# A windowed and a linear attention on one core: the same instructions emitted in another planned order

## The chip, the cores and the metric

The kernel runs on one core of a Trainium2 chip. The metric is the device time of one execution in microseconds (us); the time given for a kernel is the median of its timed runs.

## The reference, cut to what matters

Two independent attentions over 2,048 tokens of width 640 (32 heads of 20) stand side by side in the output. A is a softmax attention in which each query sees itself and the 255 keys before it; B is a linear attention with the feature map phi. All inputs are bf16.

```python
def _A_ref(x, wqkv, wo):              # S = 2048, D = 640, H = 32, Dh = 20, W = 256
    q, k, v = split(x @ wqkv)
    scores = jnp.einsum("bhqd,bhkd->bhqk", q, k) * (Dh ** -0.5)
    mask = (idx[:, None] - idx[None, :] >= 0) & (idx[:, None] - idx[None, :] < W)
    p = _softmax(jnp.where(mask[None, None], scores, -1e9), axis=-1)
    o = jnp.einsum("bhqk,bhkd->bhqd", p, v)
    return merge_heads(o) @ wo
def _B_ref(x, wqkv, wo):
    phi = lambda t: jnp.where(t > 0, t + 1, jnp.exp(t)) + 1e-6
    pq, pk = phi(q), phi(k)
    kv = jnp.einsum("bhsd,bhse->bhde", pk, v)
    z = jnp.einsum("bhsd->bhd", pk)
    o = jnp.einsum("bhqd,bhde->bhqe", pq, kv) / (jnp.einsum("bhqd,bhd->bhq", pq, z)[..., None] + 1e-6)
    return merge_heads(o) @ wo
return jnp.concatenate([a, b], axis=-1)   # (1, 2048, 1280)
```

## The kernel before

**A list of small jobs and a planner.** `build` (L317) does not write instructions in the order in which they run. It makes some 700 jobs, each with a closure that emits its instructions, the engines that may do it with an estimated duration, the jobs it depends on, and a name. `Planner.run` (L156) then plays a simple model of the chip forward in time: each engine has a clock, `LAT` is added between engines, a DMA job has an issue time, a service time and a fixed latency (the `D_...` tuples, L356 on), and eight DMAs may be under way for each kind of queue. Whichever engine is free first takes, among its ready jobs, the one with the lowest key, and the closure is called, so the planner's order becomes the program's order on that engine. The keys are in the table `TUNE`: `"name"` is a priority, and `"@name"` is the earliest time in nanoseconds at which a DMA job may be planned. Three scalars in `PRM` belong to the rules: `pvw` (how long a PV job is held back for company), `look` (how far ScalarE looks ahead for an exp) and `slack` (added to each planned landing). On the chip there are no planned times: each engine runs its fixed list, and waits with semaphores for what an instruction reads or overwrites.

**The work of A.** The 512-token tiles t = 0..3 are loaded turned (features on partitions) by `load_x` (L476; one `dma_start_transpose` of 512x640, L491, called a turned load here, names ldxA1..3), tile 0 as four row blocks that TensorE turns. `proj` (L504) makes q{t}.{i} and k{t}.{i}, each five matmuls of 128x512 (L516); the odd heads are regrouped by small DMAs on GpSimd's queue (rl1, rl2: L548, L551). `proj_v` (L565) makes v{t}.{b}.{i} (five matmuls of 128x320, L578) and copies half of each pair to other partitions through two DMAs on SyncE's queue (sw, L590 on). `attn` (L605) makes the scores as units S{t}.{g}.{u}: 32 or 48 small matmuls (L647) into one four-bank PSUM tile, of which there is one; one exp on ScalarE reads it all (L663, 128x2048, or 128x1536 for S0.g.3), VectorE multiplies masks in (L675), and PV{t}.{g} (L701, 144 instructions with their weight loads counted for t = 0, 192 otherwise) sums up the four or five units of a group g. There are 76 units. Each next unit needs the PSUM tile, so it starts when the exp before it has read it. The results go to DRAM (ow), come back in another layout (osum, oc: `a_out`, L754), and oa{t}.{b}.{hf} multiplies them with wo (`finish_rows`, L735) and stores.

**The work of B.** kB{t}.{b}.{hf} (five 128x320 matmuls, L835) with an exp and two more operations for phi make the keys' features; ten groups G{c}.{hf} (16 matmuls each, L860) sum features against the tokens (xtok0..3, plain loads); z and zt (L896 on) make the normalisers; kv and kvwo (L952, L970) form the 640x640 product with wo, which goes through DRAM (kvw, kvr); qB{t}.{c} (L1015), den (L1027) and ob{t}.{b}.{hf} (L735) make the output. The weights wvB, wo6 and wo6b (L934, L941, L942; 0.80, 0.75 and 0.15 MB) take the buffers of xtok0, xtok1 and xtok2, so their loads are issued when the last G group in TensorE's order has used these.

**Rings.** The turned tiles of A and B share three boxes in the order in which the loads are written down (A0, B0, A1, B1, A2, B2, B3, A3 and ldy0..3, B's tiles loaded again for the queries), so a turned load waits in SyncE's queue for the last reader of the box that it takes. Warm fillers without a purpose in the result (L1061 at the start, twelve of L1063 with the lowest priority) are emitted where the planner finds TensorE free. PSUM has four slots "F" for everything but scores.

**A unit and its PSUM tile, as emitted** (L639 and L663):

```python
st["s"] = mk("s", [P, 4 * SWD], F32, "S", tag="S")
...
nc.scalar.activation(out=o_, in_=i_, func=ACT.Exp, scale=scale)
```

Of the kernel before, what the change touches and what calls it, by code (L numbers as in the profile page):

```python
# [7 lines left out]
P = 128  # L8
# [6 lines left out]
PRM = {"rq": "POOL", "pvw": 4091, "look": 4707, "slack": 696, "xm": 5}  # L15
TUNE = {
    "x0n0": -288357, "@x0n0": 600, "x0n1": 22049, "@x0n1": 1123, "x0n2": 41981, "@x0n2": 2434, "x0n3": 84061, "@x0n3": 119, "ld.wq0": 76083,
    "ld.wk0": 12236, "@ld.wk0": 6060, "ld.wq1": -35479, "@ld.wq1": 3681, "ld.wk1": 6066, "@ld.wk1": 6620, "ld.wv": -505446, "@ld.wv": 5636,
    "cq0": -84337, "cq1": 2724, "cq2": 44219, "cq3": -23187, "cq4": -420730, "ck0": 5696, "ck1": -64118, "ck2": 18670, "ck3": 29291, "ck4": -26858,
    "x0t0": -132897, "x0t1": -294040, "x0t2": -85730, "x0t3": -4915, "q0.0": 19248, "q0.1": 26432, "q0.2": -6686, "q0.3": 45970, "q0.4": -489536,  # L20
    "rl1.q0": -40785, "@rl1.q0": 16932, "rl2.q0": 54695, "@rl2.q0": 13518, "k0.0": -73776, "k0.1": -51790, "k0.2": 37394, "k0.3": 113822,
    "k0.4": 46053, "rl1.k0": -502673, "@rl1.k0": 30975, "rl2.k0": -49405, "@rl2.k0": 26708, "v0.0.0": -6929, "v0.0.1": 47622, "v0.1.0": -526600,
    "v0.1.1": -444090, "sw0.0": -61952, "@sw0.0": 10936, "v0.2.0": 10862, "v0.2.1": -501633, "v0.3.0": 40518, "v0.3.1": -71548, "sw0.1": -68807,
    "@sw0.1": 9193, "ld.wkB": 25497, "@ld.wkB": 23848, "ldxB0": -246197, "@ldxB0": 26131, "ldxA1": -59032, "@ldxA1": 15091, "kB0.0.0": -45974,
    "kB0.0.1": -446546, "kB0.1.0": -18749, "kB0.1.1": -31544, "kB0.2.0": -28401, "kB0.2.1": -58682, "kB0.3.0": -6118, "kB0.3.1": -486764,
    "q1.0": -75602, "q1.1": -34298, "q1.2": 92743, "q1.3": 61377, "q1.4": -456991, "rl1.q1": -18606, "@rl1.q1": 55172, "rl2.q1": -528074,
    "@rl2.q1": 73862, "k1.0": -3303, "k1.1": -483479, "k1.2": 42406, "k1.3": -33423, "k1.4": -34976, "rl1.k1": 11630, "@rl1.k1": 46441,
    "rl2.k1": 40373, "@rl2.k1": 4611, "v1.0.0": 24902, "v1.0.1": 75996, "v1.1.0": -55369, "v1.1.1": 2908, "sw1.0": -456214, "@sw1.0": 43512,
    "v1.2.0": -35867, "v1.2.1": -288257, "v1.3.0": 33377, "v1.3.1": 46161, "sw1.1": -34319, "@sw1.1": 53419, "ldxB1": -26199, "@ldxB1": 41031,
    "kB1.0.0": -113500, "kB1.0.1": -23254, "kB1.1.0": -28925, "kB1.1.1": 46817, "kB1.2.0": -483358, "kB1.2.1": 7107, "kB1.3.0": 16553,  # L30
    "kB1.3.1": -6454, "ldxA2": -86975, "@ldxA2": 44207, "q2.0": 51284, "q2.1": -37600, "q2.2": -6714, "q2.3": 60478, "q2.4": -65006,
    "rl1.q2": -16466, "@rl1.q2": 19526, "rl2.q2": -509535, "@rl2.q2": 30153, "k2.0": -33063, "k2.1": -456351, "k2.2": -81624, "k2.3": 47673,
    "k2.4": -2355, "rl1.k2": 127476, "@rl1.k2": 117376, "rl2.k2": -21923, "@rl2.k2": 72214, "v2.0.0": 37551, "v2.0.1": 18807, "v2.1.0": -421067,
    "v2.1.1": -36145, "sw2.0": -45842, "@sw2.0": 23643, "v2.2.0": 25454, "v2.2.1": -539290, "v2.3.0": -130767, "v2.3.1": 11608, "sw2.1": -38625,
    "@sw2.1": 27245, "ldxB2": -550245, "@ldxB2": 38750, "kB2.0.0": 100598, "kB2.0.1": 10322, "kB2.1.0": -9462, "kB2.1.1": -69461, "kB2.2.0": -110719,
    "kB2.2.1": 38546, "kB2.3.0": -87349, "kB2.3.1": -486127, "ld.woA": -54728, "@ld.woA": 27767, "ldxB3": 27036, "@ldxB3": 91221, "kB3.0.0": -453951,
    "kB3.0.1": -38228, "kB3.1.0": -24615, "kB3.1.1": -37138, "kB3.2.0": -29442, "kB3.2.1": -45218, "kB3.3.0": -13993, "kB3.3.1": -71775,
    "xtok0": 104034, "@xtok0": 10388, "xtok1": -16821, "@xtok1": 51509, "xtok2": -120603, "@xtok2": 36076, "xtok3": -197007, "@xtok3": 97651,
    "G0.0": 10547, "G0.1": -17739, "G1.0": -55082, "G1.1": -8864, "G2.0": -490163, "G2.1": -324802, "G3.0": -26464, "G3.1": -33272, "G4.0": -15409,
    "G4.1": -483548, "z": 16997, "zt": -471321, "ldxA3": -19285, "@ldxA3": 88410, "q3.0": -23726, "q3.1": -37994, "q3.2": 56848, "q3.3": -265204,  # L40
    "q3.4": 52841, "rl1.q3": -78551, "@rl1.q3": 24462, "rl2.q3": -10455, "@rl2.q3": 61591, "k3.0": -41972, "k3.1": -13087, "k3.2": 65456,
    "k3.3": -26454, "k3.4": -7302, "rl1.k3": -39963, "@rl1.k3": 180268, "rl2.k3": 57329, "@rl2.k3": 9912, "v3.0.0": 29050, "v3.0.1": -43769,
    "v3.1.0": -18803, "v3.1.1": -1031, "sw3.0": -8116, "@sw3.0": 47187, "v3.2.0": 53184, "v3.2.1": -33591, "v3.3.0": 10942, "v3.3.1": -84607,
    "sw3.1": -41924, "@sw3.1": 24173, "ld.wvB": -426561, "@ld.wvB": 145679, "ld.wo6": -39687, "@ld.wo6": 30114, "kv0": -51294, "kv4": -426176,
    "kvwo0.0": 122701, "kvwo0.1": 12241, "kvwo1.0": -101551, "kvwo1.1": 31130, "kvwo2.0": -11861, "kvwo2.1": 11563, "kvwo3.0": 107146,
    "kvwo3.1": 131618, "kvwo4.0": -11166, "kvwo4.1": -50861, "kvwo5.0": 55450, "kvwo5.1": -278982, "kvw": -6720, "@kvw": 112744, "kvr": 46418,
    "@kvr": 69351, "ld.wqB": -280019, "@ld.wqB": 64126, "ow0": -429736, "@ow0": 27062, "ow1": 93906, "@ow1": 67296, "ow2": 44109, "@ow2": 53571,
    "ow3": 53864, "@ow3": 102364, "osum0": -573874, "@osum0": 76330, "oc0": -88479, "@oc0": 22414, "oa0.0.0": -82090, "oa0.0.1": -17943,
    "store": -53603, "@store": 120847, "oa0.1.0": 107388, "oa0.1.1": 50337, "oa0.2.0": -3404, "oa0.2.1": 34788, "oa0.3.0": -4230, "oa0.3.1": 37536,
    "osum1": -38603, "@osum1": 136143, "oc1": 47960, "@oc1": 56532, "oa1.0.0": -16324, "oa1.0.1": 24478, "oa1.1.0": -6962, "oa1.1.1": -12310,  # L50
    "oa1.2.0": 19872, "oa1.2.1": 25087, "oa1.3.0": -438000, "oa1.3.1": 29423, "osum2": -17457, "@osum2": 114162, "oc2": 4253, "@oc2": 130803,
    "oa2.0.0": -13955, "oa2.0.1": 10901, "oa2.1.0": -495123, "oa2.1.1": -10320, "oa2.2.0": -364531, "oa2.2.1": -12125, "oa2.3.0": -553036,
    "oa2.3.1": 21611, "osum3": 42013, "@osum3": 80849, "oc3": 59899, "@oc3": 118912, "oa3.0.0": -55744, "oa3.0.1": -244782, "oa3.1.0": -196742,
    "oa3.1.1": 41674, "oa3.2.0": -40598, "oa3.2.1": -584, "oa3.3.0": -93513, "oa3.3.1": -62120, "ldy0": 796, "@ldy0": 131627, "qB0.0": 29481,
    "qB0.1": -10081, "qB0.2": -68216, "qB0.3": -6372, "qB0.4": -46422, "den0": -33393, "ob0.0.0": -31941, "ob0.0.1": 35471, "ob0.1.0": -528525,
    "ob0.1.1": -24391, "ob0.2.0": -36065, "ob0.2.1": 27561, "ob0.3.0": -27764, "ob0.3.1": -464803, "ldy1": -13798, "@ldy1": 133257, "qB1.0": 1053,
    "qB1.1": -36459, "qB1.2": -444342, "qB1.3": -435813, "qB1.4": 56456, "den1": -388121, "ob1.0.0": -37266, "ob1.0.1": -54446, "ob1.1.0": 46384,
    "ob1.1.1": 63708, "ob1.2.0": 61437, "ob1.2.1": 91909, "ob1.3.0": 13961, "ob1.3.1": 25475, "ldy2": -531291, "@ldy2": 179542, "qB2.0": -110948,
    "qB2.1": 4978, "qB2.2": 35459, "qB2.3": 45246, "qB2.4": -18854, "den2": 89974, "ob2.0.0": -169618, "ob2.0.1": 7409, "ob2.1.0": -7287,
    "ob2.1.1": 9127, "ob2.2.0": 29090, "ob2.2.1": 55666, "ob2.3.0": 3198, "ob2.3.1": 20750, "ldy3": -581352, "@ldy3": 90810, "qB3.0": -56384,  # L60
    "qB3.1": -40973, "qB3.2": -253517, "qB3.3": -69741, "qB3.4": -66337, "den3": 30737, "ob3.0.0": -325, "ob3.0.1": 5523, "ob3.1.0": 43879,
    "ob3.1.1": 53150, "ob3.2.0": -38432, "ob3.2.1": -4618, "ob3.3.0": -75801, "ob3.3.1": -132216,
}


def KEY(name, value):
    return value


class Op:  # L70
    def __init__(self, idx, engs, emit, key, deps, mode, slots, g, rel, name, dma, cls, earliest, ni):
        self.ni = ni
# [25 lines left out]
class Planner:  # L98
    def __init__(self, slots):
        self.ops = []  # L100
        self.slots = {k: 0 for k in slots}
        self.free = {}
        self.log = []
        self.mode = "f"
        self.net = {"HW": 0, "SW": 0}
        self.lands = {"HW": [], "SW": []}
# [1248 lines left out]
```

## Time and profile before

| | |
|---|---|
| runs | 269.05, 269.86, 270.78 us; median 269.86 |
| profiled execution | 268.76 us, of which the span from the first to the last instruction is 267.0 |
| granted TensorE clock, mean over the span | 0.983 |
| TensorE | 4,117 matmul records, 248.9 us busy; 4,147 weight-load records |
| ScalarE | 204 instructions, 199.6 us busy; of these 76 exps with 141.0 us |
| VectorE | 457 instructions, 181.4 us busy |
| GpSimd | 93 instructions, 40.3 us busy |
| DMA | 36.07 MB, mean 135 GB/s |
| first and last matmul | starts at 1.27 us; ends at 262.58 us |

Times are counted from the first instruction. "Idle before" is the time that an engine stood still just ahead of an instruction, and the releaser is what ended it. "Issue" means that the engine waited for nothing the profile shows. "q8 instruction" is the DMA queue that brings TensorE's instructions: 33 packets of 16 KB. A matmul with its weight load counts as two instructions in TensorE's stream, which has 8,294 of these. A granted clock of 0.50 in a window means that TensorE ran at half speed there.

### The profile page before, as it was taken

The numbers are of one execution on the slowest core, as the hardware profiler recorded it, in microseconds if no ns is written. First come the engines' busy times: TensorE is split into PE (matmuls) and PEld (weight loads), VectorE is DVE, ScalarE is ACT, GpSimd is POOL, SyncE is SP. The second block draws the span as 40 slices with busy tenths as digits, with TensorE's granted clock in tenths as the row PEclk, the third lists the DMA queues.
The fourth block names the chain that finished last, engine by engine and source line by source line (L and its number), as shares of the span: only waits on it lengthen the run. The fifth ranks groups of instructions, "written<-read, shape, count | busy, mean of one in ns | idle before, by whom it ended". The sixth has DMA issues, their size and how long they took to land.

```text
span 267.0 us, 9518 instructions
## 1 busy us (share of the span) xinstructions
PE 248.9 (93%) x4117; PEld 149.3 (56%) x4147; DVE 181.4 (68%) x457; ACT 199.6 (75%) x204; POOL 40.3 (15%) x93
## 2 busy tenths in 40 slices
PE   8999989999999959999999999799979998999993
PEld 4754546565564635546666666655445555565672
DVE  1576758887769865768644556488789768675850
ACT  3528577897999956899786898189997797966631
POOL 5064503303060600007200000000500000000000
PEclk9999999999999997999999999799999999999998
DMA  7974969299342990001958129153996523213423
GB/s 227 337 144 147 156 193 220 67 204 215 92 146 68 150 233 8 21 23 62 260 102 133 62 47 259 47 174 94 202 155 185 182 83 117 76 50 100 160 99 104
DMA packets 52948, 36.07 MB, mean 135 GB/s; under 512 B 31702, under 2 KB 51494, under 8 KB 52902
## 3 DMA queue, kind: packets, MB, share of 16 engines
q1 hardware_dynamic: 50198, 32.39, 50.4%
q0 software_dynamic: 2048, 2.63, 5.0%
q8 instruction: 33, 0.54, 0.9%
q10 hardware_dynamic: 656, 0.41, 0.5%
q14 instruction: 13, 0.11, 0.2%
HBM read 13.90 MB, written 10.26 MB: 90 GB/s over the span
## 4 chain that ended last, share of the span: by engine, by line
PE 85%; issue 4%; ACT 3%; DVE 2%; SPq 2%; DMA 2%; ACTq 0%
PE F L735 17%; PE F L516 14%; PE S L647 10%; PE F L835 9%; PE F L860 9%; PE F L578 8%; PE F L701 7%; PE F L1015 6%; ACT p L663 3%; DMA sw<-vt 2%; PE F L1027 2%; SPq L491 1%; PE F L1061 1%; PE F L952 1%; PE F L1063 1%
## 5 line engine op out<-in xcount | busy, mean ns | idle before, releaser
L663 ACT ACTIVATE p<-S 128x2048 bf16<-128x2048 f32 x76 | 141.0, 1855 | 33.5 <-PE S L647 32.1
L675 DVE TENSOR_TENSOR p<-p,strip 128x256 bf16<-128x256 bf16 (+2 forms) x140 | 49.3, 382 | 17.0 <-ACT p L663 16.0
L809 ACT ACTIVATE e<-F 128x320 bf16<-128x320 f32 (+1 forms) x52 | 25.3, 498 | 6.3 <-PE F L835 3.1
L835 PE MATMUL F<-wkB,xT 128*128 128x320 bf16 x160 | 28.6, 307 | 0.2 <-issue 0.2
L548 POOL DMA_DIRECT2D odd<-even x32 | 16.5, 522 | 80.2 <-ACT even L415 58.3
L417 DVE CAST osb<-F 128x320 bf16<-128x320 f32 x41 | 19.4, 487 | 13.3 <-PE F L735 11.3
L551 POOL DMA_DIRECT2D odd<-st x32 | 17.9, 566 | 69.1 <-DVE st L417 55.7
L578 PE MATMUL F<-wv,xT 128*128 128x320 bf16 x160 | 28.0, 303 | 0.2 <-DVE e L813 0.2
L735 PE MATMUL F<-woA,oc 128*128 128x320 bf16 x160 | 27.1, 306 | 0.1
L516 PE MATMUL F<-xT,wk 128*128 128x512 bf16 x93 | 25.0, 379 | 0.7 <-issue 0.5
L735 PE MATMUL F<-kvwo,pq 128*128 128x320 bf16 x160 | 24.9, 299 | 0.2 <-DMA kvwo<-kvd 0.2
L1015 PE MATMUL F<-xT,wqB 128*128 128x512 bf16 x89 | 23.3, 380 | 1.1 <-issue 0.9
L417 DVE CAST ost<-F 128x512 bf16<-128x512 f32 x21 | 13.9, 688 | 14.9 <-PE F L701 14.9
L860 PE MATMUL F<-pk,xtok 128*128 128x320 bf16 x160 | 24.0, 300 | 0.0
L701 PE MATMUL F<-p,sw 64*32 64x320 bf16 (+3 forms) x720 | 21.6, 254 | 2.5 <-issue 1.9
L516 PE MATMUL F<-xT,wq 128*128 128x512 bf16 (+1 forms) x99 | 23.0, 358 | 1.0 <-issue 0.8
L701 PE MATMUL F<-p,vt 64*32 64x320 bf16 (+3 forms) x720 | 21.8, 254 | 0.7 <-issue 0.7
L417 DVE CAST even<-F 128x512 bf16<-128x512 f32 x24 | 16.5, 689 | 7.3 <-PE F L516 7.2
L647 PE MATMUL S<-odd 20*64 20x320 bf16 (+4 forms) x720 | 16.9, 261 | 4.1 <-issue 3.9
L835 PEld LDWEIGHTS <-xT 128*128 128x128 bf16 x160 | 15.1, 100 | 9.0 <-issue 1.0
L735 PEld LDWEIGHTS <-pq 128*128 128x128 bf16 x160 | 15.2, 98 | 8.3 <-issue 0.8
L578 PEld LDWEIGHTS <-xT 128*128 128x128 bf16 x160 | 15.0, 99 | 8.2 <-issue 1.4
(88 smaller groups left out, 309.1 us busy)
## 6 DMA issues: line engine op xcount, KB each, us to landing
out_dram<-osb SPq DMA_DIRECT2D x32, 160.0 KB, 2.0
OD<-ost SPq DMA_DIRECT2D x32, 128.0 KB, 2.4
xtok<-in_B_x_dram SPq DMA_DIRECT2D x4, 640.0 KB, 5.8
oc<-OD SPq DMA_DIRECT2D x4, 640.0 KB, 5.3
odd<-even POOLq DMA_DIRECT2D x32, 48.0 KB, 6.3
sw<-vt SPq DMA_DIRECT2D x16, 87.0 KB, 3.7
odd<-st POOLq DMA_DIRECT2D x32, 32.0 KB, 3.3
wv<-in_A_wqkv_dram SPq DMA_DIRECT2D x1, 800.0 KB, 6.7
```

Source lines behind the costliest of these rows:

```text
L417: nc.vector.tensor_copy(out=dst, in_=src)
L516: nc.tensor.matmul(ps[:, a:b], lhsT=w[:, kt, i, :], rhs=xb["t"][:, kt, a:b], start=(kt == 0), stop=(kt == KT - 1))
L578: return lambda ps: nc.tensor.matmul(ps[:], lhsT=xb["t"][:, kt, bb * P : bb * P + P], rhs=rhs_(), start=(kt == 0), stop=(kt == KT - 1))
L647: nc.tensor.matmul(st["s"][64 * i : 64 * i + 64, o0 : o0 + b - a], lhsT=kb["t"][32 * j : 32 * j + Dh, sl, ko : ko + 64], rhs=qb["t"][32 * ...
L663: nc.scalar.activation(out=o_, in_=i_, func=ACT.Exp, scale=scale)
L675: nc.vector.tensor_tensor(out=x, in0=x, in1=mkv[:, None, :].to_broadcast([P, 4, 64 * w]), op=ALU.mult)
L701: nc.tensor.matmul(O[i][32 * j : 32 * j + 32, a:b], lhsT=lhsT, rhs=pb["t"][64 * i : 64 * i + 64, o0 : o0 + b - a], start=(cnt == 0), stop= ...
L735: return lambda ps: nc.tensor.matmul(ps[:], lhsT=lhs(c), rhs=rhs(c, hf), start=(c == 0), stop=(c == KT - 1))
L809: nc.scalar.activation(out=eb["t"][:, 0:n], in_=ps[:], func=ACT.Exp)
L835: return lambda ps: nc.tensor.matmul(ps[:], lhsT=xb["t"][:, kt, b * P : (b + 1) * P], rhs=R["wkB"][:, kt, hf * HALF : (hf + 1) * HALF], st ...
L860: return lambda ps: nc.tensor.matmul(ps[:], lhsT=R["xt", tb // 4][:, tb % 4, c * P : (c + 1) * P], rhs=R["pk", tb // 4][:, tb % 4, hf * HA ...
L1015: return lambda ps: nc.tensor.matmul(ps[:], lhsT=R["wqB"][:, kt, :].rearrange("p (f c) -> p c f", c=KT)[:, c, :], rhs=xb["t"][:, kt, :], s ...
```

## The change

Every emitted instruction and every transfer stays what it was: the same 8,294 loads and matmuls, 76 exps, 439 VectorE and 202 ScalarE operations of the planned jobs, and the same DMAs, 16 sw transfers on SyncE's queue in both. What differs is the order in which each engine gets them, since the planner has other numbers:

- the whole table `TUNE` (every priority and every earliest time), and `pvw`, `look` and `slack`;
- the model of transfers: one server for both kinds of queue instead of two, another landing formula, and other costs for every kind of DMA;
- sw is planned on SyncE's queue, where it was emitted before too, although the planner had it on GpSimd's; `load_x` loses a branch that was not taken; `heat` tells the planner its count of instructions.

```diff
-PRM = {"rq": "POOL", "pvw": 4091, "look": 4707, "slack": 696, "xm": 5}
+PRM = {"rq": "POOL", "pvw": 2241, "look": 3200, "slack": 509, "xm": 5, "sq": "SP"}
 TUNE = {
...
-DMA_LEAD, DMA_LANES = 700, 8
+DMA_LEAD, DMA_TAIL, DMA_LANES = 1190, 300, 8
...
-        self.net = {"HW": 0, "SW": 0}
+        self.net = 0
...
-                q = "SW" if e == "POOL" else "HW"
-                for _ in range(n):
-                    self.net[q] = max(done + DMA_LEAD, self.net[q]) + svc
-                    land = self.net[q] + fix - DMA_LEAD
-                    self.lands[q].append(land)
+                q = self.lands["SW" if e == "POOL" else "HW"]
+                for i in range(n):
+                    self.net = max(t + dur * i // n + DMA_LEAD, self.net) + svc
+                    land = max(self.net, t + dur * (i + 1) // n + DMA_TAIL) + fix
+                    q.append(land)
...
-    D_XT5 = (3500, 1, 4200, 1150)
+    D_XT5 = (2850, 1, 3300, 1800)
...
-        D_RL1 = (950, 1, 350, 2100)
+    D_RL1 = (520, 1, 708, 1106) if RQ == "POOL" else (740, 1, 540, 893)
...
+    SQ = PRM.get("sq", RQ)
+    D_SWAP = (560, 1, 560, 1100) if SQ == "POOL" else (630, 1, 419, 965)
...
-                        nc.sync.dma_start(out=sws[slot][64:128, :, :], in_=vts[slot][0:64, :, 336:684])
+                        q_of(e).dma_start(out=sws[slot][64:128, :, :], in_=vts[slot][0:64, :, 336:684])
...
-                o = dma(sw, D_SWAP, -4990, [...], name=f"sw{t}.{hb}", eng=RQ)
+                o = dma(sw, D_SWAP, -4990, [...], name=f"sw{t}.{hb}", eng=SQ)
```

The emitted orders compare as follows where they differ most. SyncE's queue, before: ..., ldxB1, ow, ow, ldxA2, xtok1, ow, ow, ldxB2, ow x4, oc0, osum0, ow, ow, ldxA3, ldxB3, ...; after: ..., ldxB1, ow, ow, xtok2, sw1.0, ldxB2, ldxA2, ow, ow, sw1.1, ow, ow, ldxB3, osum0, oc0, xtok1, ow, ow, xtok3, sw2.0 (first half), ow, ow, ldxA3, .... Near the end of B's sums both have wvB, wo6, wo6b in a row.

TensorE at the last G group, before: G0.0 (its long piece of 30 instructions starts at 157.33 us) with S2.3.0, z, S2.3.1, zt, pieces of tile 1's output projection, S2.3.2, PV2.2, kv4 and kv0; after: G4.0, G1.0, G3.0 with S2.3.3, S2.3.4 and S3.0.0 between their pieces, then S3.0.1, PV2.3, pieces of tile 1's output projection, S3.0.2, z, S3.0.3, kv0, zt, kv4. TensorE between S0.3.3 and S1.0.3, before: the rest of kB1.2.0, PV0.3, and projections of tile 2; after: PV0.3 and kB1.0.1 to kB1.3.1, with the first projection of tile 2 (k2.4) just behind S1.0.3. Over the whole stream the units come in the same sequence, and so do the PVs.

## The prediction

> **What bounds the kernel now.** First the page's shares, clock and chain.
>
> ```profile
> PE 248.9 (93%) x4117; PEld 149.3 (56%) x4147; DVE 181.4 (68%) x457; ACT 199.6 (75%) x204; POOL 40.3 (15%) x93
> PEclk9999999999999997999999999799999999999998
> PE 85%; issue 4%; ACT 3%; DVE 2%; SPq 2%; DMA 2%; ACTq 0%
> ```
>
> TensorE is the bound. With the same instructions in another order only three things can move the end: time in which TensorE stands ("issue" is 4% of the chain, 11 us), stretches of halved clock (the two 7s), and the waits that the order makes. Next the chain around the two longest halts (start, length, what):
>
> ```profile
> 97.25 0.21 PE S L647 x13
> 97.47 2.92 issue
> 100.39 0.36 PE S L647 x11
> ...
> 165.50 1.11 PE F L701 x78
> 166.61 1.92 issue
> 168.53 0.53 PE F L701 x16
> ```
>
> Both halts fall inside a row of like matmuls, so no tile is waited for. By count they stand before the 3,010th and the 5,570th instruction of TensorE's stream: exactly ten blocks of 256 apart, and q8 brings 33 packets for 8,294 instructions. I call every 256th place an edge. The transfers by queue (packets, MB, share of 16 engines), first in 85.8 to 97.4 us, then in 97.4 to 99:
>
> ```profile
> q1 hardware_dynamic: 5147, 1.31, 81.8%
> q0 software_dynamic: 255, 0.33, 16.8%
> q14 instruction: 2, 0.02, 0.8%
> ...
> q1 hardware_dynamic: 497, 0.49, 97.2%
> q8 instruction: 1, 0.02, 5.6%
> ```
>
> For 11.6 us q8 got nothing while the others filled the engines. TensorE passed the edge before at 92.65, which asks for the block wanted at 97.47; its packet ran from 97.46 for 1.44 us, and TensorE went on 1.5 us later. The other long halt is alike: packet wanted at about 163, started 165.98. Ahead of it stood three loads that SyncE issued together (1.7 MB):
>
> ```profile
> 157.94 0.38 SPq L934 DMA_DIRECT2D wvB<-in_B_wqkv_dram  x1
> 158.49 0.42 SPq L941 DMA_DIRECT2D wo<-in_B_wo_dram  x1
> 159.03 0.41 SPq L942 DMA_DIRECT2D wo6b<-in_B_wo_dram  x1
> ```
>
> By stage (window, length, PE, PEld, DVE, ACT, POOL busy, granted clock, DMA share, GB/s): each halt is followed by one window of 3.41 us at half clock.
>
> ```profile
> 97.69:101.10 3.41, 0.71 (x15) 0.45 (x16) 0.81 (x3) 0.33 (x2) 0.00 (x0) 1.00 0.71 254
> 101.10:104.52 3.42, 3.42 (x22) 1.76 (x27) 1.33 (x4) 1.92 (x2) 0.00 (x0) 0.50 0.03 8
> 165.96:169.37 3.41, 1.50 (x79) 1.04 (x64) 0.28 (x1) 1.83 (x1) 0.00 (x0) 1.00 0.24 70
> 169.37:172.78 3.41, 3.41 (x31) 2.96 (x29) 2.02 (x5) 0.00 (x0) 0.00 (x0) 0.50 0.25 82
> ```
>
> Last the score units, from ScalarE's timeline. One PSUM tile serves all 76, so a unit starts only when the exp before it is done:
>
> ```profile
> 53.13 1.88 ACT L663 ACTIVATE p<-S 128x2048 bf16<-128x2048 f32 x1 [0.46 <-PE S L647]
> 54.90 0.43 ACT L809 ACTIVATE e<-F 128x320 bf16<-128x320 f32 x1
> 55.76 1.88 ACT L663 ACTIVATE p<-S 128x2048 bf16<-128x2048 f32 x1 [0.42 <-PE S L647]
> ```
>
> From a unit's start to its exp 0.50, the exp 1.88, to the next unit 0.04 to 0.16: a cycle of 2.45 us (least seen 2.42 and 2.47; 2.02 with the 1.45 us exp of tile 0's narrow units). Here the starts are 2.63 apart: TensorE has enough between them.
>
> **The change, part by part.** I laid the changed order out with TensorE's durations from rows of before: a unit 0.43 us, five 128x512 matmuls 1.08, five 128x320 0.685, a PV 1.42 (tile 0: 1.035), z 1.23, a filler 0.22. This work is the same in both orders.
>
> *Edges moved.* Undisturbed, from an edge passed (209.79) to the block after it ready (212.95) takes 3.1 us. Before, the least work between edges is 2.47, 2.87 and 3.54 us, since they lie in a PV or unit (many short instructions). The halts at edges 11, 21, 25, 27 and 29 are 2.92 + 1.92 + 0.24 + 0.41 + 0.70 = 6.2 us. In the new order the least is 4.26. If every fetch ran at once, no halt would be left: −6.2.
>
> *A fetch behind queued loads.* In the nine cases of before in which transfers filled the engines, q8's packet started when those queued ahead had run. After, wvB, wo6 and wo6b are issued 0.6 us into the long piece of G3.0, as they were into that of G0.0; before, TensorE went on 168.53 − 157.33 = 11.2 us after that piece's start. Edge 22 now falls in PV2.3, behind the issue; its block is wanted at edge 23, the end of S3.0.3, after 7.76 us of work. A new halt of 11.2 − 7.8 = 3.4 us, in front of kv0, which needs wvB anyway. Bounds: 0 if the fetch is served between the loads, 5.0 if it waits for all of wo6b's landing (167.56). I take +3.4, as the old halt is the same three loads in the same order. The Trainium skill ("Runtime: NRT & Kernel Launch", section "Instruction fetch mechanics") agrees on blocks of 256 instructions but calls the crossing mostly hidden; the 2.92 and 1.92 above say otherwise, and by that sentence this term would be near 0.
>
> *Other edges behind transfers* (after edges 5, 7, 17 and 24, soon after a turned load's or several small transfers' issue): nothing to +2.5; +0.4, since a packet at 27.90, 1.6 us after the issue of a turned load (26.30), came without delay.
>
> *Half clock.* A window at half clock loses 3.41/2 = 1.7. Two before; one after, behind the halt of 3.4. −1.7. Idle of 0.88 in a window (193.26 to 196.67) halved nothing; idle of 1.91 and 2.70 did.
>
> *Score cadence.* Where TensorE's work between two unit starts is below the cycle, it waits. Before: S2.3.3 (1.67), S3.1.0 (2.30), S3.1.1 (1.57), S3.2.1, S3.2.2; shortfall 2.6 us. After: S0.2.2 2.19, S0.3.2 2.18, S0.3.3 1.39, S1.0.0 2.28, S1.0.1 1.67, S1.0.2 1.66 (only kB1 groups are at hand, as ldxA2 now stands behind ldxB2), shortfall 2.9; S3.0.4 2.28, S3.1.0 1.39, S3.1.1 2.12, S3.1.3 1.27, shortfall 2.7. Net 5.6 − 2.6 = +3.0, bounds +2 and +4.5 (phi's exps between: 0.43 each on ScalarE, where they don't fit). Behind a waiting unit stand the masks and the PV, which come two units later, so nothing else is late.
>
> *Transfers moved.* The wait for sw at 34.41 (0.63) goes, as sw now stands ahead of ldxB0 in SyncE's queue: −0.6. wk1 goes behind xtok0 (640 KB), with 3 us of cover; nothing, without cover at most xtok0's 2 us. ldxA2 behind ldxB2: k2.4 needs it 9.3 us of work later, and the cadence waits add 2; turned loads took 5.8 to 8.7 us alone, 10.1 to 12.5 in pairs: 0, at most +1. ldxA3 8.2 us ahead of q3.1: +0.2, at most +2. The last stretch and the tail (4.4 us after the last matmul) are alike.
>
> *Sum:* −6.2 + 3.4 + 0.4 − 1.7 + 3.0 − 0.6 + 0.2 = −1.5. The profiled execution (268.76, span 267.05) becomes 267.3, span 265.5. The runs' median lies 1.1 above that execution; on its scale I forecast 268.4.
>
> **Rivals.**
> *B: the fetch isn't held up by the 1.7 MB.* For: q8 is a queue of its own, with one packet at a time. Against: the nine late packets. Then 3.4 and the last half-clock window go: 268.4 − 3.4 − 1.7 = 263.3. The Trainium skill ("DMA: Bandwidth & Descriptors", section "Queues, rings and completion order") speaks for it: an engine takes turns between the queues that have work, a packet each. By that rule, 97.46 should have been 92.65; the trace disagrees at least there.
> *C: the fetches wait for turned loads too; slower.* Edge 5 comes 1.3 us after the issue of ldxB2, edge 7 1.8 us after that of ldxB3. If a fetch issued so shortly behind one starts at its landing (8.5 us after issue; up to 12.5 for the pair B2, A2), TensorE goes on 2.85 us after that: 52.7 + 8.5 + 2.85 = 64.05 against edge 6 at 59.77, 4.3 late; 65.1 + 8.5 + 2.85 = 76.45 against edge 8 at 73.29, 3.2 late. 268.4 + 7.5 = 275.9, one alone about 272.5 with a halved window. A packet more than 2.9 us behind edge 5 or 3.6 behind edge 7 becomes a halt; 4.0 behind both brings the kernel back to 269.9. For: a packet wanted at 56.2, with ldxA2 issued at 51.19, came at 60.49. Against: 27.90.
> *D: the halts are not the edges'* and stay with the work wherever it goes: only cadence and sw count, 269.86 + 3.0 − 0.6 = 272.3. Against: the exact 2,560 instructions.
>
> **How the numbers follow.** Forecast 0.46 (own range 266 to 271: the fetch's 0 to 5.0, the cadence's +2 to +4.5), B 0.26, C 0.20, D 0.08. One per cent, 2.7 us, is about what a measurement tells from no change: below 267.2 or above 272.6. Faster: 0.14 of the forecast's and 0.25 of B's, 0.39; slower: 0.02, C 0.16 and D 0.03, 0.21; same 0.40. The range 262 to 274 leaves out C's upper part (0.13) and B's lowest (0.04).
>
> **What would show it.** q8's packet about 8 us after wvB's issue and a halt of 2 to 5 us in front of kv0, with one 0.50 window behind it; no halt ending on "issue" above 0.5 us elsewhere; unit starts 2.45 apart with waits ahead of S1.0.2, S1.0.3, S3.1.1 and S3.1.4. Wrong if q8 keeps coming during the three loads (B), if a halt stands 256 instructions behind edge 5 or 7 (C), or if halts stand off the edges (D).

## The result and the profile after

| | before | after |
|---|---|---|
| runs, same job | 269.05 to 271.06, median 270.32 us | 266.28 to 267.09, median 266.98 us |
| profiled execution | 268.76, span 267.05 | 267.09, span 265.29 |
| last matmul ends | 262.58 | 259.63 |

The ratio is 0.9876 (95% interval 0.9831 to 0.9920): 1.2% faster. A second comparison on another chip gave 0.9893 (0.9833 to 0.9953). The forecast for the median was 268.4, inside a range of 262 to 274; 266.98 was measured, 1.4 us less. For the profiled execution it was 267.3, and 267.09 was measured. The kernel before spreads more from run to run (266.4 to 271.2 in the comparisons with other kernels below) than the one after (266.2 to 267.1), which is why the medians lie 3.3 us apart and the two profiled executions 1.7. Runs of a slower state, the longest at 273.6 us, are left out of these spreads and of all ratios.

The page after, in the same parts as before (line numbers are now those of the changed kernel: the scores' L647 is L635, the exp's L663 is L651):

```profile
PE 248.2 (94%) x4118; PEld 149.6 (56%) x4147; DVE 182.4 (69%) x457; ACT 198.7 (75%) x204; POOL 40.4 (15%) x93
...
PEclk9999999999999999999999999977999999999999
...
PE 84%; ACT 7%; issue 4%; DVE 3%; ACTq 0%; DVEq 0%
```

TensorE is still the bound and still 4% of the chain is "issue", but the two 7s of the clock now stand side by side: one place instead of two. The chain there (start, length, what):

```profile
172.88 0.43 PE S L635 x15
173.31 3.04 issue
176.35 0.42 PE S L635
176.77 0.65 PE F L723 x2
```

That is S3.0.3, held before its very last matmul. It is the only halt on "issue" above 0.2 us in the whole stream; before there were six, 6.45 us in sum. The transfers by queue (packets, MB, share of 16 engines) from wvB's issue on, 165.7 to 173.5 us, and then from 173.5 to 175:

```profile
q1 hardware_dynamic: 1328, 1.65, 86.0%
...
q1 hardware_dynamic: 404, 0.41, 91.7%
q8 instruction: 1, 0.02, 5.3%
```

Nothing came on q8 while nearly all of the three loads ran; its packet started at 173.58, which is 7.80 us after wvB's issue at 165.78 (8.04 before). The edge that asks for it, in PV2.3, was passed at about 168.7. The windows behind it (window, length, PE, PEld, DVE, ACT, POOL busy, granted clock, DMA share, GB/s):

```profile
172.57:175.99 3.42, 0.58 (x25) 0.31 (x24) 0.97 (x3) 0.26 (x1) 0.00 (x0) 1.00 0.81 204
175.99:179.40 3.41, 3.05 (x31) 2.54 (x31) 1.58 (x5) 1.88 (x1) 0.00 (x0) 0.50 0.04 11
179.40:182.82 3.42, 3.42 (x37) 2.35 (x36) 2.03 (x4) 1.75 (x1) 0.00 (x0) 0.50 0.17 51
```

Two windows at half clock follow the one halt, where one had been forecast. And the waits in front of score units, which the view of before does not have at all (engine, line, releaser: us in total, times, longest):

```profile
PE S L635 <- ACT p L651: 2.7, 7, 0.7
```

### The profile page after: what moved, and what is told of

The parts are those of the page before. It is cut to its first block, busy times and chain, and to the rows that moved or that the text cites. A ratio compares the mean times of both kernels' runs of the same rounds, so it can differ in the third digit from the quotient of the medians.

```text
span 265.3 us, 9525 instructions
## 1 busy us (share of the span) xinstructions
PE 248.2 (94%) x4118; PEld 149.6 (56%) x4147; DVE 182.4 (69%) x457; ACT 198.7 (75%) x204; POOL 40.4 (15%) x93
## 4 chain that ended last, share of the span: by engine, by line
PE 84%; ACT 7%; issue 4%; DVE 3%; ACTq 0%; DVEq 0%
PE F L723 17%; PE F L504 16%; PE S L635 9%; PE F L848 9%; PE F L566 9%; PE F L1003 7%; PE F L823 7%; PE F L689 6%; ACT p L651 6%; PE F L1015 2%; PE F L1049 1%; PE F L940 1%; ACT e L797 1%; PE F L1051 1%; DVE p L663 1%
## 5 line engine op out<-in xcount | busy, mean ns | idle before, releaser
L651 ACT ACTIVATE p<-S 128x2048 bf16<-128x2048 f32 x76 | 141.1, 1857 | 25.8 <-PE S L635 23.3
L663 DVE TENSOR_TENSOR p<-p,strip 128x256 bf16<-128x256 bf16 (+2 forms) x140 | 49.2, 381 | 17.4 <-ACT p L651 16.8
L823 PE MATMUL F<-wkB,xT 128*128 128x320 bf16 x160 | 26.7, 300 | 0.2 <-DVE p L663 0.2
L566 PE MATMUL F<-wv,xT 128*128 128x320 bf16 x160 | 26.4, 300 | 0.1
L1003 PE MATMUL F<-xT,wqB 128*128 128x512 bf16 x90 | 24.1, 380 | 1.1 <-issue 0.7
L504 PE MATMUL F<-xT,wq 128*128 128x512 bf16 (+1 forms) x99 | 24.0, 358 | 0.8 <-issue 0.3
L413 DVE CAST even<-F 128x512 bf16<-128x512 f32 x26 | 17.9, 689 | 9.0 <-PE F L504 8.3
L723 PE MATMUL F<-kvwo,pq 128*128 128x320 bf16 x160 | 23.9, 299 | 0.2 <-DVE pq L1034 0.2
L635 PE MATMUL S<-even 20*64 20x320 bf16 (+4 forms) x720 | 16.7, 263 | 5.7 <-issue 3.0
L723 PEld LDWEIGHTS <-oc 128*128 128x128 bf16 x160 | 15.3, 100 | 11.9 <-issue 4.7
L689 PE MATMUL F<-p,vt 64*32 64x320 bf16 (+3 forms) x720 | 21.1, 254 | 0.0
L566 PEld LDWEIGHTS <-xT 128*128 128x128 bf16 x160 | 14.8, 98 | 8.6 <-issue 1.2
```

The source lines that it names most:

```text
L413: nc.vector.tensor_copy(out=dst, in_=src)
L504: nc.tensor.matmul(ps[:, a:b], lhsT=w[:, kt, i, :], rhs=xb["t"][:, kt, a:b], start=(kt == 0), stop=(kt == KT - 1))
L566: return lambda ps: nc.tensor.matmul(ps[:], lhsT=xb["t"][:, kt, bb * P : bb * P + P], rhs=rhs_(), start=(kt == 0), stop=(kt == KT - 1))
L635: nc.tensor.matmul(st["s"][64 * i : 64 * i + 64, o0 : o0 + b - a], lhsT=kb["t"][32 * j : 32 * j + Dh, sl, ko : ko + 64], rhs=qb["t"][32 * ...
L663: nc.vector.tensor_tensor(out=x, in0=x, in1=mkv[:, None, :].to_broadcast([P, 4, 64 * w]), op=ALU.mult)
L689: nc.tensor.matmul(O[i][32 * j : 32 * j + 32, a:b], lhsT=lhsT, rhs=pb["t"][64 * i : 64 * i + 64, o0 : o0 + b - a], start=(cnt == 0), stop= ...
```

## The experiments

Theory 1: the next block of 256 instructions is asked for at an edge of TensorE's stream, its packet waits for the transfers queued ahead, and nearly all that the new order gains is that fewer edges meet such transfers. Its rivals: the halts belong to the work around them; q8 is served in turn; or the new order is better in itself.

Several kernels below keep one of the two orders and move single jobs in it. For that the planner's choices are collected, some are shifted, and only then emitted. An entry of `MOVES` such as `('ldxB3', 0, 'ow1', 3)` puts the first job named ldxB3 right behind the fourth one named ow1:

```diff
-            if not dry:
-                o.emit(e)
+            seq.append((o, e))
...
+        for what, nth, where, wth in MOVES:
+            x = seq.pop(find(what, nth))
+            seq.insert(find(where, wth) + 1, x)
+        if not dry:
+            for o, e in seq:
+                o.emit(e)
```

**after_edges_192: the edges moved, nothing else.**

```diff
-            for i in range(n * NQ // w):
+            for i in range(104 if w == NQ else n * NQ // w):
                 if w == NQ:
-                    nc.tensor.matmul(psum(g)[:], lhsT=warm[:, 0:P], rhs=warm[:], start=True, stop=True)
+                    nc.tensor.matmul(psum(g)[:, 0:39], lhsT=warm[:, 0:P], rhs=warm[:, 0:39], start=True, stop=True)
```

> The kernel after, with the eight warm-up matmuls of 512 columns cut into 104 of 39 columns: about the same warm-up work, 192 more instructions at the very start of TensorE's stream, so every 256-instruction edge falls 192 instructions earlier in the work (64 later by the next edge); nothing else is changed. Theory 1 (a block's fetch is asked for at the edge before and waits for the transfers queued ahead): an edge now lies ahead of wvB's effect differently, the next one comes later, in kv0, and the halt of 3.04 us at S3.0.3 becomes one of about 1.3 us (0.5 to 2) at kv0; too short to halve the clock, so both half-clock windows (1.7 us each) go: about 262 us. Rival (the halt belongs to the work around S3.0.3 or to the waiting for data): it stays at S3.0.3 with 3 us and the time at 267.

Measured: 263.98 us, ratio 0.9821 (0.9759 to 0.9882). From its chain:

```profile
175.29 0.54 PE F L940 x9
175.84 1.48 issue
177.32 0.54 PE F L940 x6
```

L940 is kv0: the halt left S3.0.3 and came to the place and nearly the size that theory 1 named (1.48 for 1.3). The profiled execution still had one half-clock window behind it, which I had not expected of so short a halt, and a second halt of 0.52 in a PV. 192 more small instructions in the warm-up made the median about 3 us less (2.4 less than in after_again below). By the ratios, into which the spread of the kernel before enters, it is 1.5 to 1.9 us, and their intervals overlap.

**after_wo_late: the suspected transfers taken away from ahead of the fetch.** `MOVES = [('ld.wo6', 0, 'ow2', 7)]`

> The kernel after, with the job that loads wo and wo6b (0.9 MB) put behind the next two ow transfers in SyncE's queue, so that only wvB (0.8 MB) stands ahead of the fetch that edge 22 asks for; TensorE's order and its edges are unchanged. Theory 1: the packet comes when wvB has run, about 5.1 us after its issue instead of 7.8, TensorE is held at S3.0.3 for 0.5 us (0 to 1) instead of 3.04, the two half-clock windows go, and kvwo may wait up to 1 us for wo: about 261.5 us. Rival (q8 is served in turn with the other queues, or the fetch is slow by itself): the packet still comes about 7.8 us after wvB's issue, the halt stays 3 us, 267.

Measured: 261.15 us, ratio 0.9733 (0.9670 to 0.9796), against 0.9876 for the changed kernel: 5.8 us less than its median, 5.2 less than in after_again, and about 4 by the ratios. SyncE's issues in the timeline, the page's clock by slices, and the chain at S3.0.3:

```profile
166.04 0.39 SPq L936 DMA_DIRECT2D wvB<-in_B_wqkv_dram  x1
170.23 1.27 SPq L725 DMA_DIRECT2D OD<-ost  x2
171.59 0.39 SPq L943 DMA_DIRECT2D wo<-in_B_wo_dram  x1
```

```profile
PEclk9999999999999999999999999999999999999998
```

```profile
173.10 0.04 issue
173.15 0.43 PE S L649 x16
173.58 0.38 PE F L737 x2
```

With wvB alone ahead, q8's packet came at 170.07, 4.0 us after wvB's issue instead of 7.8; S3.0.3 runs through, and no window in the middle is halved. That one job was worth 3.0 us of halt and two windows of 3.41 us at half speed.

**before_edges_128: the edges of the old order moved.** The same edit as in the first experiment, 72 matmuls of 56 columns.

> The kernel before, with the eight warm-up matmuls cut into 72 of 56 columns: 128 more instructions at the start, so that every edge falls half a block earlier in the same work; no other change. Theory 1: the halt at S1.2.3 (2.92) goes and a longer one comes at the end of PV1.1 (about 6.6, as that block is asked for at the beginning of the time in which the engines are full and wanted earlier), one of about 2.9 comes at S0.3.3, the one in PV2.2 moves to its beginning (about 3), the small ones at S3.2.2, S3.3.2 go: 12.7 us of halts instead of 6.2, and one half-clock window more: about 277 us. Rival (halts belong to the work or to data): 268.8 with the halts where they were.

Measured: eight runs between 263.96 and 273.06 us, too far apart for a ratio, so only the places of the halts count. Chains of its profile:

```profile
39.14 1.46 issue
...
62.19 2.23 issue
...
98.40 0.88 PE F L701 x67
99.28 1.87 issue
101.15 0.29 PE F L701 x5
...
142.71 1.27 issue
```

The halts at S1.2.3 and in PV2.2 are gone, and others stand at edges of the moved count: in S0.1.3, in S0.3.3, ten instructions before the end of PV1.1, and in a G group. So they go with the count, not with the work. Their sizes were badly forecast: 1.87 for 6.6 in PV1.1, none for about 3 at the beginning of PV2.2, and two, in S0.1.3 and in the G group, that were not forecast at all; 6.8 us in sum for 12.7. The earlier halts put off the issue of ldxA3 from 86.62 to 92.25, so its transfer met another fetch. One idle time on "issue" of 0.27 us, in a PV of tile 3, did stay with the work when the edges moved (197.48 before, 200.12 here); it is not an edge's.

**before_two_loads_late: two jobs of the old order moved.** `MOVES = [('ldxB3', 0, 'ow1', 3), ('ld.wo6', 0, 'store', 4)]`

> The kernel before, with two jobs of SyncE's queue put later and nothing else changed: the turned load ldxB3 behind the two ow1 transfers that followed it, and the loads of wo and wo6b behind the store that followed them. Theory 1: the block wanted at S1.2.3 is fetched once ldxA3 has run (about 95.1 instead of 97.46), the halt there falls from 2.92 to about 0.5; the one in PV2.2 falls from 1.92 to 0.3 or less; both half-clock windows go; kvwo waits 1 to 2 us for wo: 268.8 - 2.4 - 1.6 - 3.4 + 1.5 = about 263 us. If that holds, two moved jobs bring more than the whole new order. Rival (the order of the work is what made the kernel after faster): 268 to 269.

Measured: 265.78 us (three runs at 265.14 to 265.91, one at 269.30), ratio 0.9894 (0.9819 to 0.9969), level with the new order. Both long halts are gone, as theory 1 has it. In one point it was too strict: the block wanted at S1.2.3 came at 93.48, 0.8 us after its edge, and not only when ldxA3 had landed (95.05). Much of the gain went into a new wait that I had put at 1 to 2 us:

```profile
161.95 7.15 DMA wo6b<-in_B_wo_dram
169.09 0.14 issue
169.23 0.49 PE F L984
```

kvwo stood 3.73 us for wo6b, issued at 161.95 behind a store that waits for its data, and two windows were halved behind that wait.

**before_wo_on_act** and **before_wo_later_on_act**: wo and wo6b from ScalarE's queue, at two places. `MOVES = [('ldxB3', 0, 'ow1', 3), ('ld.wo6', 0, 'E2.3.0', 0)]` (the second with `'E2.3.1'`), and

```diff
-            nc.sync.dma_start(out=R["wo6"][:], in_=B_wo[0:600, :].rearrange("(g r) n -> r g n", r=120))
-            nc.sync.dma_start(out=R["wo6b"][:], in_=B_wo[520:640, :])
+            nc.scalar.dma_start(out=R["wo6"][:], in_=B_wo[0:600, :].rearrange("(g r) n -> r g n", r=120))
+            nc.scalar.dma_start(out=R["wo6b"][:], in_=B_wo[520:640, :])
```

> The kernel before with ldxB3 behind the two ow1 transfers, as in before_two_loads_late, and wo and wo6b issued from ScalarE's queue right behind the exp of unit S2.3.0 (about 157.8 us), just ahead of the edge in S2.3.1, so that the fetch goes first and the loads are there when kvwo wants them (165.5). Theory 1 (the gain of the new order is the absence of halts behind transfers): no halt at S1.2.3 or PV2.2, no wait of kvwo above 1 us, no half-clock window in the middle: 265.8 - 3.7 - 3.4 = 258.7 us, 258 to 261, as good as the new order without its halt (261.15). Rival (the new order is better in itself): no better than 264.

Measured: 264.21 us, ratio 0.9818 (0.9735 to 0.9901). I had misjudged when that exp ends: wo was issued at 155.67, 2 us ahead of the edge, which was passed at about 157.8; the packet came at 161.37, and PV2.2 was held again:

```profile
161.06 1.11 PE F L715 x78
162.17 1.74 issue
163.90 0.88 PE F L715 x14
```

> As before_wo_on_act, with wo and wo6b issued from ScalarE's queue one exp later (behind that of S2.3.1, about 158.3 us instead of 155.67). In before_wo_on_act they were issued ahead of the edge in S2.3.1 and the packet came only at 161.37, with a halt of 1.74 us in PV2.2 and a half-clock window. Theory 1: with wvB alone ahead the packet comes at about 158.4, as in before_two_loads_late; no halt in PV2.2, no half-clock window, and kvwo, wanted at 165.5, waits at most 0.5 us for wo: 264.2 - 1.7 - 1.7 = 260.8 us (260 to 262.5), level with the new order without its halt (261.15). Rival: the new order is better in itself, 263 or more.

Measured: 260.92 us, ratio 0.9713 (0.9644 to 0.9783). Issued at 157.50, behind the edge (about 157.05), wo lets the packet go at 157.71, 3.7 us earlier for a load issued 1.8 us later; no halt in PV2.2, no wait of kvwo for wo, no halved window. The old order with two jobs moved (0.9713) is then level with the new order with one job moved (261.15, 0.9733), within intervals of about 2 us either way. The rival "better in itself" falls as far as these can tell.

**before_later_edges_32:** the same, with 24 warm-up matmuls of 170 columns.

> As before_wo_later_on_act, and the eight warm-up matmuls cut into 24 of 170 columns, 32 more instructions at the start, so that every edge falls 32 instructions earlier. In the layout of the old order the least work between two edges grows from 2.47 to 3.95 us. Theory 1: the small halts on issue (0.42 at S3.3.2, 0.74 and 0.27 in a PV of tile 3) go: about 259.5 us. The edge before S1.2.3 is crossed earlier too, so up to 0.6 us may come back there. Rival (these small halts aren't the fetch's): 260.8.

Measured: 259.83 us, ratio 0.9659 (0.9597 to 0.9721), the lowest of all. The small halts at S3.3.2 (0.59) and at the start of a PV (1.10) became one of 0.77. The step of 1.1 us from before_wo_later_on_act is within the intervals. The kernel beats both others, by 9.2 us the one before (268.99) and by 6.6 us the one after (266.39) in the same job.

**after_again:** 

> The changed kernel itself, unchanged, beside the two above on one chip: 267 us, with the halt of about 3 us at S3.0.3.

Measured: 266.39 us, with a halt of 3.03 us at the same place.

**after_wo_late_short_exp** and **after_wo_late_short_exp2:** after_wo_late with ten exps halved.

```diff
+                        w_ = 2 * n if short else 4 * n
+                        if short:
+                            nc.gpsimd.memset(pb["t"][:, w_ : 4 * n], 1.0)
-                        o_, i_ = pb["t"][:, 0 : 4 * n], st["s"][:, 0 : 4 * n]
+                        o_, i_ = pb["t"][:, 0:w_], st["s"][:, 0:w_]
```

> The kernel after with wo and wo6b late, and with the exp of ten units (S0.3.2, S1.0.0 to S1.0.3, S3.0.4 to S3.1.3) doing the first half of its columns only; the other half of p is set to one by GpSimd, so these probabilities are left out. Theory (the waits in front of units come from the length of the exp cycle, 2.45 us): the cycle becomes about 1.5, the waits of 0.55, 0.67 and 0.55 us in front of S1.0.0, S1.0.2 and S1.0.3 and of 0.28, 0.24 and 0.37 at S3.0.4 to S3.1.4 go: 2.6 us less, about 258.5 us. Rival (the waits are TensorE's for slots or operands, the exp only seems to end them): they stay above 1.5 us in sum, 261.

Measured: 261.63 us, ratio 0.9730 (0.9654 to 0.9806). TensorE's waits for an exp (above 0.2 us each) fell from 2.66 to 0.55 us, and that one follows an exp that was not shortened: the waits do come from the exp. But no time was gained (258.5 was forecast), because GpSimd's MEMSETs got in VectorE's way (start, length, instruction, from the timelines of the two engines):

```profile
58.28 2.75 POOL L667 MEMSET p<- 128x1024 bf16 x3
```

```profile
58.39 2.74 DVE L821 TENSOR_SCALAR e<-e 128x320 bf16<-128x320 bf16 x1
```

> As after_wo_late_short_exp (ten units whose exp does the first half of its columns only), but the other half of p is set to one by VectorE instead of GpSimd. In the run before, the waits in front of the units behind a shortened exp went (2.66 us to 0.55, which follows an exp that was not shortened), but one TENSOR_SCALAR of VectorE took 2.74 us (58.39 to 61.13) beside three MEMSETs of GpSimd (58.28 to 61.03), PV0.3 waited 1.44 us for it and the clock was halved in one window. Theory (exp cycle): without GpSimd in the way the waits stay away, PV0.3 waits under 0.3 us, no half clock: 261.15 - 2.1 = about 259 us. Rival (the units' waits hide the next limit, phi on VectorE): PV0.3 or kB1 waits 1 us or more again and the time stays at 261.

Measured: 267.40 us, ratio 0.9960 (0.9922 to 0.9999). The theory's time failed, and so did its rival's. The waits for the exp stayed away, but ten MEMSETs of 0.91 us on VectorE cost far more than they freed: TensorE waited 2.42 us for phi's last operation (pk) and 3.96 for copies of kvwo, and two windows were halved. In this run VectorE is the limit in these two stages; what a shorter exp alone would bring stays open, as both ways to leave it out burdened VectorE.

**after_wo_late_tail** and **after_wo_late_split_stores:** the tail. In the first the last of 32 stores goes out on ScalarE's queue, in the second the first eight stores are split in two.

> The kernel after with wo and wo6b late, as in after_wo_late, and the very last of the 32 stores issued from ScalarE's queue, right behind the copy on ScalarE that it waits for, instead of from SyncE's. In the kernels with the new order that last issue takes 1.7 to 1.9 us on SyncE, in those with the old one 0.33, while instruction packets run on q14. Theory T (SyncE's own instruction block ends there): the store goes out 1.4 us earlier, the time from the last matmul to the end falls from 5.6 to about 4.2 us: about 259.8 us. Rival (the end of the program costs that anyway, or the issue is slow for the fetch of TensorE's last block): the tail stays 5.3 to 5.6, 261.

> The kernel after with wo and wo6b late, and the first eight of the 32 stores issued as two halves of 64 rows each: eight more instructions in SyncE's stream, around 100 to 200 us, where SyncE has time. Theory T (the 1.4 us by which the last store's issue is longer in the new order is a block edge of SyncE's own instruction stream, which lies at its last store there and behind it in the old order, whose last store comes five of its instructions earlier): the long issue moves to a store four to eight places earlier, the tail after the last matmul falls from 5.6 to about 4.4 us: 260 us. Rival (the issue is slow because TensorE's stream ends and its last block is fetched then): the last store's issue stays at 1.7 us and the tail at 5.6, 261.2.

Measured: 261.72 us, ratio 0.9726 (0.9666 to 0.9786), and 261.61, ratio 0.9751 (0.9692 to 0.9810): no gain. The long issue did go, to 0.37 on ScalarE and to 0.33 on SyncE with eight instructions more ahead of it. But none of SyncE's last sixteen issues became long in its place (0.57 at most), as theory T has it, so a block edge of SyncE's own stream is not shown. And the tail stayed 5.55 and 5.57 us, now with a wait of SyncE of 1.2 to 1.7 us in its closing list of semaphores. The traces show for what: the store ahead of the last one. Sixteen semaphore updates tell of its landing; fifteen had come by 1.7 us after the end of the last matmul, the sixteenth at 3.25 and 3.38. In the profiles of the change that sixteenth came at 2.18 before and 3.10 after. So two things stand side by side in the new order, the long issue and this late update, and taking away the first leaves the second. Why the issue is long and the update late in the new order is open.

## Why the prediction was right, step by step

Differences of the two profiled executions:

| step | forecast | measured |
|---|---|---|
| halts of the old order go | −6.2 | −6.45, of which 0.27 is not at an edge |
| new halt behind the three loads | +3.4 | +3.04 |
| other edges behind transfers | +0.4 | 0 |
| half clock | −1.7 | two windows in both, about −0.2 (an estimate) |
| waits for the exp above 0.2 us, net | +3.0 | +2.4 |
| sw, ldxA3 | −0.4 | −0.6 |
| other waits of TensorE (den, kvwo, fillers) | 0 | −0.5 |
| tail behind the last matmul | 0 | +1.2 |
| what is left over: TensorE's busy time, small gaps | 0 | −0.6 |
| span | −1.5 | −1.8 |

**The fetch, both signs.** This is the step that carried the forecast, and the runs bear it out: the halts followed the edges when only the count was changed (after_edges_192, before_edges_128), and the packet followed the transfers when only these were moved (7.8 us after wvB's issue with three loads ahead, 4.0 with one). The traces of all the runs together hold 26 halts of TensorE on "issue" above 0.2 us. Counted with TensorE's semaphore instructions, 22 of them stand at place 193 or 194 of a block of 256, and the other four are the 0.27 us that stay with a PV.

The new halt came out by its terms too: TensorE went on 11.2 us after the start of G3.0's long piece (165.17 to 176.35), as forecast, and the block was wanted 8.1 us after it, for 7.76. One reading was too strong: that a packet starts when the transfers queued ahead have run. It can start before they land: at 97.46 with ldxB3 landing at 99.95 (before), at 93.48 with ldxA3 landing at 95.05 (before_two_loads_late). And the 3.1 us of an undisturbed fetch are 3.0 in the rows (edge 26 at 209.7, TensorE on again at 212.71); no term rests on that.

**Rival B (served in turn)** fell: 4.9 us from the edge to the packet while 1.27 MB went past, where the edge before (162.2) had its packet after 0.8. The Trainium skill ("DMA: Bandwidth & Descriptors", section "Queues, rings and completion order") says that an engine takes turns between queues by packets; by that a packet of 16 KB would not stand behind whole loads, and here the trace disagrees. The Trainium skill's other sentence, that crossing a block edge is mostly hidden ("Runtime: NRT & Kernel Launch", section "Instruction fetch mechanics"), holds for the changed order with one exception of 3.04 us.

**Rival C (turned loads)** was right that a fetch can be late behind turned loads, but not that it starts at their landing. Edge 5's packet came about 2 us after the edge, at 56.50, 4.4 us after ldxB2's issue and not 8.5. The packet for edge 6, passed at about 61.1, came at 65.26, ahead of the landing of ldxA2 (issued 55.54, landed 66.56): 4.1 us after the edge where the next edge left 8.9, so nothing halted. Edge 7's came at 69.10, 0.7 us after ldxB3's issue (68.40), without delay. C's sum was also short: its 275.9 leaves out the halved windows that halts of 3.2 and 4.3 us would bring, and for one of them with such a window its terms give 273.3 to 274.4, not 272.5.

**Rival D** fell with the moved edges; only the 0.27 us in a PV of tile 3 behave as it says.

**Half clock** is the step that failed: I took one window for one halt. The halt of 3.04 us lay across the border of two windows of 3.41, with 2.84 idle in one and 0.36 in the next, and was followed by two: the second of them was itself halved, and because TensorE still stood in it for 0.36, so was the one behind it. The wait of 3.73 in before_two_loads_late had two as well, with 2.48 idle in one window and 1.25 in the next; the halts of 1.74 (before_wo_on_act) and 1.48 (after_edges_192) had one. So two windows were halved in both kernels, where two and one were forecast. What that is worth is an estimate: half of TensorE's busy time in them, 3.05 + 3.42 after and 3.42 + 3.41 before, or −0.2. The term was mis-sized by 1.5 us.

**The exp cycle** was right in its net, but by luck: forecast 5.6 after and 2.6 before, measured 2.4 after (2.7 with the shorter ones) and none before. At S1.0.0 to S1.0.3 the waits came nearly as listed (0.55, 0.13, 0.67, 0.55, for shortfalls of 0.63, 0.17, 0.78 and 0.79). In the stage of tile 3 only 0.60 of 2.7 came. The halved clock and kvwo's own waits (0.50 and 0.27) may have filled the time in which units were to wait, and den's and kvwo's (0.75 and 0.58) that of the old order, but this is not shown: without a halved clock (after_wo_late) the waits of tile 3 were still only 0.88.

**The tail** was called alike from the order of the stores; it was not. That miss of 1.2 us and the 1.5 of the clock were offset by the gains that I had left at nothing (−0.5, −0.6) and the terms taken too high, so that the sum of −1.5 lies this close to −1.8 is partly luck.

**What the sum did not say:** the new order as such was worth nothing measurable. Without their long fetch halts the two orders stand at 261.15 and 260.92, the old one with 1.7 us of short ones left.

## What to carry to other kernels

In a long unrolled stream like this one, count TensorE's instructions, semaphore instructions included: every 256th is an edge, and from there until the next the block must come through the same DMA engines as the data. Look for halts on "issue" inside a row of like matmuls, find the last q8 packet, and see which large loads were issued ahead of it; then move these loads behind the edge, or the edge with a few cut-up fillers, before planning the work anew. Lay out all edges before you move them: 128 instructions more in the old order only traded its halts for others. And leave a halved clock its own line in the sum: here a halt of 3 us cost 5 to 6 (after_wo_late against the changed kernel).

## What the runs showed of the hardware that was not expected

A GpSimd MEMSET can hold an operation of VectorE for its whole length: a TENSOR_SCALAR of 128x320 that takes 0.24 us elsewhere took 2.74 (58.39 to 61.13) beside three MEMSETs of 128x1024 on GpSimd (58.28 to 61.03). Not every operation was held: beside the MEMSET of 56.83 to 57.81 a TENSOR_TENSOR of 128x768 took 0.54 and a SCALAR_TENSOR_TENSOR 0.48, as without it (0.55 and 0.48 in after_wo_late). The Trainium skill ("SBUF — State Buffer", section "SBUF: two separate sides") says that GpSimd shares a pair of ports with some of VectorE's operations, those in a two-port mode above all, as an exclusive lock for a whole instruction. The trace agrees with such a lock; in which mode each operation ran it does not show.

The granted clock punishes idleness by the window and sooner than I took it. In all these traces it changes at borders that lie 3.41 us apart, and what counts is how long TensorE stood within one window. Up to the last matmul, all 11 windows at full clock with 1.67 us or more of idle time were followed by a halved one, and none with 1.46 or less. In between it went both ways: 1.48 (after_edges_192) brought a halved window, 1.54 (before_two_loads_late, 33.11) did not, and what decides there is open. A halved window through which TensorE worked (at most 0.06 idle, 12 cases) was the last; one in which it stood again was followed by another, with 1.25 idle (before_two_loads_late), 0.36 (the changed kernel) and 0.38 (after_again).
